# The front part of an attention and MLP block in another order: keys ahead of maxima, idle products in TensorE's waits, 50 maxima at the loop's entry and a lead of five half cycles

## The chip, the core and the metric

The kernel runs on one core of a Trainium2 chip. Time is device microseconds (us) of that core for one launch. TensorE (PE) multiplies, VectorE (DVE) reduces, ScalarE (ACT) takes exponentials and copies, GpSimd (POOL) does elementwise work, SyncE (SP) issues nearly all DMAs. Each engine runs its own queue strictly in the order in which it was written, and so does SP's queue of DMAs.

## The reference

```python
mod = (_silu(c) @ w_mod).reshape(1, 6, 1, -1)          # sa, ca, ga, sb, cb, gb
h = _layernorm(x) * (1 + ca) + sa                       # x: 1 x 2048 x 512
q = (h @ wq) as 32 heads of 16;  k = h @ wk;  v = h @ wv   # one key and value head for all 32
p = softmax(q k^T / 4);  x = x + ga * ((p v) @ wo)
h = _layernorm(x) * (1 + cb) + sb
x = x + gb * (gelu(h @ w1 + b1) @ w2 + b2)              # w1: 512 x 1376
```

All in float32, with wide spreads, so the kernel splits operands into a high and a low part and multiplies three times.

## The kernel before

**Units.** Attention is done in 64 units. A unit is 256 rows of queries and four heads; eight units (u = 8b to 8b+7) make one block b of rows. The four heads stand as two halves s = 0 and 1 of the partitions (rows 0 to 63 and 64 to 127 of the query tile `qst`), with j = 0 and 1 inside a half. Four `qst` buffers turn.

**Two passes over the scores.** The softmax takes the true maximum of each row. So each score is made twice: once as an `m` product (line 516), rows of queries in the partitions, which DVE reduces to a maximum (line 521); and once as an `e` product (line 596), keys in the partitions, from which ACT takes the exponential (line 597). A unit has 32 `m` products and 32 `e` products. The maximum goes into the `e` product itself: it is written, as a high and a low part (`mh`, `ml`), into rows 48 and 49 of each half of `qst`, where the keys `ks` hold -1. Between a unit's last `m` product and its first `e` product lies this chain, `put_max`: DVE reduces the parts (`mm`, line 570) and transposes them (`turned`, 571); POOL gathers and splits them (`mt`, `mh`, `ml`; lines 565, 131, 138); four DMAs (line 560, for s = 1 and then s = 0) bring them into `qst`. The steps are put into the program at set numbers of clock ticks after the last maximum: `reduce` at the start of the next four ticks, `gather` one tick later, `send` four ticks after `reduce`. For u = 8 and 9 `reduce` isn't put off.

**The loop.** After the front part a loop runs over pairs of key tiles, four pairs to a unit. A pair holds eight `e` products, eight `m` products of a later unit, 32 `acc` products (probabilities by values, line 608) and a batch of projection or MLP products (lines 186 and 192); it takes four clock ticks. How many `m` products stand ahead is set by `lead`: at the start of unit u, `first[u + 1] + 4 * LEAD` maxima have been issued, that is all of unit u and 4 * LEAD of the next. `LEAD_0` does the same for the first unit. DMAs are written where the code reaches them: `load_q(u + 1)` (six DMAs that fill another `qst` buffer) when half of a unit's maxima are done, and once per block of rows, in the second unit after the block's end (u = 9, 17, 25, 33, 41, 49, 57), a group that fetches the block's sums and outputs (`rsum`, `drs`, eight `os`, one `x`).

**A wait put early.** A DMA that a product needs soon is noted with `heed`; some ticks later an `acc` product is made to wait for it, so that the `e` products need not. Where no such product comes first, the `e` product itself waits.

**The front part.** Ahead of the loop stand: statistics and normalisation of four blocks of 512 rows (`stats1`, `xhat1`), transposes (`tp`), `mod1` (scale, shift, split on ACT and POOL into `big..H` and `big..L`), the key and value products `kps` of each block (12 products), `kv_out`, `low_k` and `repeat_k`, which fill `ks`, the first two projections of queries, the last part of the modulation (`modl`), and the first maxima. `SLOTS` is the written order: each entry gives how many `m` products to issue (`chunk`) and which steps of other work follow. `FIRST_MAX` gives the order of the first two units' maxima by 512 keys: (unit, key block). Between them an `m` product waits only for its operands and for one of three PSUM banks, which DVE's reduce frees. Before the first `m` product four products that nobody reads (`idle`, `keep_warm`) are already there.

Of the kernel before, what the change touches and what calls it, by code (L numbers as in the profile page):

```python
# [14 lines left out]
P = 128  # L15
# [3 lines left out]

GELU_R = 0.044715 ** 0.5  # L20

LEAD = 6
LEAD_0 = 6
FIRST_MAX = ((0, 0), (1, 0), (0, 1), (1, 1), (0, 2), (0, 3), (1, 2), (1, 3))
SLOTS = ((4, "keys 1", "keys 1"), (2, "keys 1", "keys 1"), (2, "low 1", "heads 2"), (2, "heads 2", "k 1"), (2, "heads 2"), (2, "heads 2", "v 0"),
# [4 lines left out]
MAX_WAIT = (1, 4)  # L30
QBUFS = 4
PREP = 4
# [15 lines left out]
def raw(ap):  # L48
    return ap.bitcast(F32)
# [3 lines left out]
def adaln_mqa_mlp(  # L53
# [270 lines left out]
    wqH = att.tile([P, KD, D], F32R, name="wqH", tag="gH")  # L324
    wqL = att.tile([P, KD, D], F32R, name="wqL", tag="gL")

    def prep_wq(g):
        gs = slice(g * P, (g + 1) * P)
        for j in range(2):
            src = wqf[:, :, gs].rearrange("p k (a j r) -> p k a j r", j=2, r=16)[:, :, :, j, :]  # L330
            dh = wqH[:, :, gs].rearrange("p k (a r j) -> p k a j r", j=2, r=16)[:, :, :, j, :]
            dl = wqL[:, :, gs].rearrange("p k (a r j) -> p k a j r", j=2, r=16)[:, :, :, j, :]
            nc.scalar.copy(dh, src)  # L333
            nc.gpsimd.tensor_tensor(out=dl, in0=src, in1=raw(dh), op=ALU.subtract)

    hts = {}
    hts_stats = {}
# [61 lines left out]
    def repeat_k(b):  # L399
        cols = slice(b * BQ, (b + 1) * BQ)  # L400
        nc.scalar.copy(ks[96:112, cols], raw(ks[32:48, cols]))
# [27 lines left out]

    def qproj(b, g):  # L430

        ps = psum.tile([P, BQ], F32, name=f"qps{b}_{g}", tag="v" if g else "x")
        yield from mm3(ps, qpairs(b, g), 3, 1)
        qH, qL = qtiles(b, g)
        if g == 0:
            nc.scalar.copy(qH, ps)
            nc.vector.tensor_tensor(out=qL, in0=ps, in1=raw(qH), op=ALU.subtract)
        else:
            q32 = pro.tile([P, BQ], F32, name=f"q32_{b}_{g}", tag="h32", bufs=4)
            nc.scalar.copy(q32, ps)  # L440
            split(qH, qL, q32, act, pool)
        send_q(b, g, qH, qL)
        yield -2
# [30 lines left out]
    def load_q(u):  # L474

        b, Q = units[u]
        r0, w = blocks[b]
        qst = qsts[u] = qbufs[u % QBUFS]
        h, g, a0 = r0 // BQ, Q // 2, (Q % 2) * 2
        cols = slice(r0 % BQ, r0 % BQ + w)  # L480
        assert (h, g) in sent

        for s in (1, 0):
            low, high = (dq[h][g][part, a0 + s][:, :, cols] for part in (1, 0))
            n = 6 if s else 8
# [51 lines left out]
    def put_max(u, mx):  # L537

        T = blocks[units[u][0]][1] // P
        qst = qsts[u]
        if not mms:
            for i in range(2):
                mms.append(att.tile([P, 32], F32, name=f"mm{i}"))
                nc.gpsimd.memset(mms[i], 0.0)
        mm = mms[u % 2]
        turned = att.tile([P, 32], F32, name=f"turned{u}", tag="turned", bufs=2)
        if u == 0:
            pad(att, 256, "pad7")  # L550
        mt = att.tile([4 * T, P], F32, name=f"mt{u}", tag="mt", bufs=2)
        mh = att.tile([4 * T, P], F32R, name=f"mh{u}", tag="mh", bufs=2)
        ml = att.tile([4 * T, P], F32R, name=f"ml{u}", tag="ml", bufs=2)

        def send():
            for s in (1, 0):
                for r, src in ((48, mh), (49, ml)):
                    dst = qst[64 * s + r:64 * s + r + 1].rearrange("p j (t n) -> p (j t) n", n=P)
                    ring = nc.scalar if u == 0 and s else nc.sync
                    heed(ring.dma_start(out=raw(dst), in_=raw(src[2 * T * s:2 * T * (s + 1), :].unsqueeze(1))), 5)  # L560
            placed.add(u)

        def gather():
            for g in range(0, P, 32):
                nc.gpsimd.tensor_scalar(out=mt[:, g:g + 32], in0=turned[g:g + 4 * T, :], scalar1=1.0, scalar2=0.0,  # L565
                                        op0=ALU.mult, op1=ALU.add)
            split(mh, ml, mt, nc.gpsimd, nc.gpsimd)

        def reduce():
            nc.vector.tensor_reduce(out=mm[:, :4 * T], in_=mx, axis=AX.X, op=ALU.max)  # L570
            nc.vector.transpose(out=turned, in_=mm)  # L571
            later(MAX_WAIT[0], gather)
            later(MAX_WAIT[1], send)


        if NQ <= u < NQ + 2:
            reduce()
        else:
            later((0 - clock[0]) % 4 + 1, reduce)
# [631 lines left out]

    def chunk(n):
        for _ in range(n):
            mp.step(mp.done % 2)

    act, dve, pool = nc.scalar, nc.vector, nc.gpsimd

# [43 lines left out]
    def q_group():  # L1261
        for i in range(KD):
            next(projections[0])
            if i == KD - 1:
                next(projections.pop(0))
            yield

    def one(fn, *args):
        fn(*args)
        yield  # L1270
# [34 lines left out]
    h1 = heads(1)  # L1305
    run(h1, 2)

    def last_h(t):
        if t == QT - 1:
            run(h1)  # L1310

    stats1(3, last_h)
    load_mods(2)
    repeat_k(0)
    run(xhat1(2, act))
    run(xhat1(3, act))
    work = {"keys 1": keys(1), "heads 2": heads(2), "heads 3": heads(3), "q 1": q_group(), "keys 2": keys(2), "keys 3": keys(3),
            "v 0": one(v_out, 0), "v 1": one(v_out, 1), "v 2": one(v_out, 2), "v 3": one(v_out, 3), "rows": late_rows(),
            "low 1": one(low_k, 1), "low 2": one(low_k, 2), "low 3": one(low_k, 3), "k 1": one(repeat_k, 1), "k 2": one(repeat_k, 2), "k 3": one(repeat_k, 3), "load": one(load_q, 2),
            "wq 1": one(prep_wq, 1), "wq 2": one(prep_wq, 2), "wq 3": one(prep_wq, 3)}  # L1320
    for n, *names in SLOTS:
        chunk(n)
        for name in names:
# [209 lines left out]
```

## Time and profile before

| | |
|---|---|
| median of 3 runs | 1579.97 us (1578.32 to 1580.15) |
| the profiled execution | 1579.71 us, its span 1577.9 us |
| mean granted TensorE clock | 0.997 |
| PE, DVE, ACT, POOL busy | 1554.7, 1403.8, 1204.3, 695.3 us |
| first `m` product, first `e` product | 34.13 us, 79.75 us |

Times on a profile's rows are us from the span's start. A row of the timeline has start, duration, engine, line, operation, output <- inputs, shapes and count; in brackets stands the idle time of the engine just before it and what ended it. In the table of stages a row has the stage, its length, the busy time of PE, weight loads, DVE, ACT and POOL with the number of instructions, the granted clock, and the DMA engines' share and GB/s. Matmuls overlap, so a busy PE isn't PE at its peak.

### The profile page before, as it was taken

To read this page: it belongs to the slowest core of one execution; us is meant where nothing else is said; L and a number is where in the kernel's file an instruction comes from. 1 tells how busy PE (TensorE), PEld (TensorE's weight loads), DVE (VectorE), ACT (ScalarE), POOL (GpSimd) and SP (SyncE) were. 2 spreads that over 40 slices of the span, in tenths; PEclk is the share of its full clock that TensorE was granted. 3 is DMA by queue.
4 is the path that set the end of the run, shared out by engine and by line. 5 is a ranking of instruction groups with operands and counts; after the bars stand their busy time and mean duration, and the time that the engine had idled before them with its cause. 6 is when DMAs were issued, how large, how long until landed. Compare 5 with 4: busy or idle time off the path is not lost.

```text
span 1577.9 us, 43469 instructions
## 1 busy us (share of the span) xinstructions
PE 1554.7 (99%) x17506; PEld 1040.3 (66%) x17506; DVE 1403.8 (89%) x2491; ACT 1204.3 (76%) x2418; POOL 695.3 (44%) x1253
## 2 busy tenths in 40 slices
PE   5999999999999999999999999999999999999999
PEld 3466655667767676667766677676766677676767
DVE  6899999999999999999999999999999999999715
ACT  5477777788877887778877887778877788778863
POOL 4345447447422472245523463334712465224731
PEclk8999999999999999999999999999999999999999
DMA  7236323313021120312112130212112030221341
GB/s 250 83 110 203 121 81 91 100 36 105 20 61 63 59 82 22 93 33 94 46 44 83 44 99 19 76 48 86 56 32 93 27 107 31 62 76 49 100 141 54
DMA packets 80858, 121.48 MB, mean 77 GB/s; under 512 B 16186, under 2 KB 55354, under 8 KB 80400
## 3 DMA queue, kind: packets, MB, share of 16 engines
q1 hardware_dynamic: 80640, 118.70, 23.2%
q8 instruction: 137, 2.24, 0.6%
q14 instruction: 65, 0.53, 0.1%
q10 hardware_dynamic: 16, 0.00, 0.0%
HBM read 91.00 MB, written 26.88 MB: 75 GB/s over the span
## 4 chain that ended last, share of the span: by engine, by line
PE 95%; ACT 3%; DVE 1%; DMA 0%; issue 0%; POOL 0%; SPq 0%; ACTq 0%; DVEq 0%
PE acc L608 32%; PE e L596 20%; PE m L516 18%; PE w1ps L192 8%; PE w2ps L192 6%; PE wops L192 3%; PE qps L192 2%; ACT p L597 2%; PE w2ps L186 1%; PE w1ps L186 1%; PE tp L192 1%; DVE mx L521 1%; PE kps L163 1%; PE wops L186 0%; PE modr L288 0%; DMA xt<-in_A_x_dram 0%
## 5 line engine op out<-in xcount | busy, mean ns | idle before, releaser
L521 DVE TENSOR_REDUCE mx<-m 128x1 f32<-128x512 f32 x2048 | 1270.6, 681 | 98.9 <-PE m L516 90.3
L597 ACT ACTIVATE p<-e 128x512 f32<-128x512 f32 x2048 | 1067.1, 601 | 290.5 <-PE e L596 200.2
L516 PE MATMUL m<-ks,qst 64*128 64x512 f32 x2048 | 828.4, 431 | 6.4 <-DVE ve L204 4.9
L596 PE MATMUL e<-qst,ks 64*128 64x512 f32 x2048 | 731.5, 412 | 2.1 <-ACT wqH L333 1.3
L608 PE MATMUL acc<-p,va 128*32 128x256 f32 x8192 | 548.3, 385 | 0.0
L516 PEld LDWEIGHTS m<-ks,qst 64*128 64x128 f32 x2048 | 367.2, 184 | 103.4 <-DVE mx L521 82.2
L596 PEld LDWEIGHTS e<-qst,ks 64*128 64x128 f32 x2048 | 357.6, 184 | 112.6 <-ACT p L597 102.0
L608 PEld LDWEIGHTS acc<-p,va 128*32 128x32 f32 x8192 | 214.2, 109 | 216.9 <-issue 113.2
L192 PE MATMUL w1ps<-h2H,w1t 64*128 64x256 f32 x1232 | 236.1, 288 | 0.0
L192 PEld LDWEIGHTS w1ps<-h2H,w1t 64*128 64x128 f32 x1232 | 184.0, 185 | 31.7 <-issue 22.2
L565 POOL TENSOR_SCALAR mt<-turned 8x32 f32<-8x32 f32 x256 | 53.2, 208 | 339.0 <-DVE turned L571 326.9
L192 PE MATMUL w1ps<-h2L,w1t 64*128 64x256 f32 x616 | 169.3, 275 | 0.0
L192 PE MATMUL w2ps<-w2H,gH 64*128 64x256 f32 (+1 forms) x556 | 162.3, 296 | 0.0
L192 PE MATMUL w2ps<-w2L,gH 64*128 64x256 f32 (+1 forms) x556 | 156.6, 283 | 0.0
L192 PE MATMUL w2ps<-w2H,gL 64*128 64x256 f32 (+1 forms) x556 | 155.1, 283 | 0.0
L192 PEld LDWEIGHTS w1ps<-h2L,w1t 64*128 64x128 f32 x616 | 113.5, 184 | 0.0
L192 PEld LDWEIGHTS w2ps<-w2H,gH 64*128 64x128 f32 x556 | 101.6, 184 | 10.8 <-issue 4.9
L192 PEld LDWEIGHTS w2ps<-w2H,gL 64*128 64x128 f32 x556 | 101.8, 184 | 2.3
L192 PEld LDWEIGHTS w2ps<-w2L,gH 64*128 64x128 f32 x556 | 102.4, 184 | 1.4
L957 POOL TENSOR_SCALAR tt<-tt 128x256 f32<-128x256 f32 x77 | 31.0, 403 | 144.8 <-ACT tt L956 144.8
L192 PE MATMUL wops<-woH,onH 64*128 64x256 f32 x224 | 67.8, 303 | 0.0
L192 PE MATMUL wops<-woL,onH 64*128 64x256 f32 x224 | 62.2, 277 | 0.0
(233 smaller groups left out, 1602.7 us busy)
## 6 DMA issues: line engine op xcount, KB each, us to landing
w1t<-dw SPq DMA_DIRECT2D x82, 512.0 KB
qst<-dq SPq DMA_DIRECT2D x128, 64.0 KB
do<-oc SPq DMA_DIRECT2D x63, 128.0 KB
dw<-w1s SPq DMA_DIRECT2D x11, 512.0 KB
xt<-in_A_x_dram SPq DMA_DIRECT2D x4, 1024.0 KB
dq<-qH SPq DMA_DIRECT2D x16, 256.0 KB
dq<-qL SPq DMA_DIRECT2D x16, 256.0 KB
qst<-dq SPq DMA_DIRECT2D x128, 32.0 KB
```

Of the source, the lines that this page charges most:

```text
L163: nc.tensor.matmul(ps, a, b_, start=begin and n == 0, stop=end and n == last)
L186: nc.tensor.matmul(ps, a, b_, start=first_, stop=last_)
L192: nc.tensor.matmul(ps, a[rows], b_[rows], start=first_ and s == begin, stop=last_ and s != begin)
L516: nc.tensor.matmul(m, qsts[u][rows, j, t * P:(t + 1) * P], ks[rows, kc * 512:(kc + 1) * 512], start=True, stop=True)
L521: nc.vector.tensor_reduce(out=self.mx[u][:, i, kc:kc + 1], in_=m, axis=AX.X, op=ALU.max)
L565: nc.gpsimd.tensor_scalar(out=mt[:, g:g + 32], in0=turned[g:g + 4 * T, :], scalar1=1.0, scalar2=0.0, op0=ALU.mult, op1=ALU.add)
L596: nc.tensor.matmul(e, ks[rows, kt * P:(kt + 1) * P], rhs, start=True, stop=True)
L597: nc.scalar.activation(ptiles[u, K][:, j, s, :], e, AF.Exp, scale=0.25)
L608: ins = nc.tensor.matmul(accs[u][32 * cidx:32 * cidx + 32, :], va[:, kt, :], rhs, start=kt == 0, stop=kt == NKT - 1)
L957: nc.gpsimd.tensor_scalar(out=tt, in0=tt, scalar1=1.0, scalar2=1.0, op0=ALU.mult, op1=ALU.add)
```

## The change

Four things change together.

1. The order of the front part: `SLOTS` and `FIRST_MAX` are new. Unit 0's maxima go ahead of unit 1's; the first sixteen `m` products come four of a half at a time; the key products of the blocks stand ahead of the maxima that don't need them. The second projection of queries moves from the end of the front part to the wait before the first `m` product, and its weights are split on POOL alone; block 3's `xhat1` moves from ACT to DVE; unit 0's `gather` goes from POOL to DVE; `load_q` of units 0 and 1 takes s = 0 first.
2. Products that nobody reads (`warm`) are put between the first maxima: 12, and then 1 or 2 at a time, 23 in all.
3. The loop is entered with 50 maxima instead of 56 (`LEAD_0` 4.5).
4. `LEAD` is 5 instead of 6.

```diff
-LEAD = 6
-LEAD_0 = 6
-FIRST_MAX = ((0, 0), (1, 0), (0, 1), (1, 1), (0, 2), (0, 3), (1, 2), (1, 3))
-SLOTS = ((4, "keys 1", "keys 1"), (2, "keys 1", "keys 1"), (2, "low 1", "heads 2"), (2, "heads 2", "k 1"), (2, "heads 2"), (2, "heads 2", "v 0"),
...
+LEAD = 5
+LEAD_0 = 4.5
+FIRST_MAX = ((0, 0), (1, 0), (0, 1), (0, 2), (0, 3), (1, 1), (1, 2), (1, 3))
+SLOTS = ((3, "warm"), (1, "keys 1", "warm"), (2, "keys 1", "x 3", "warm"), (2, "keys 1", "x 3", "warm"), (2, "keys 1", "x 3", "warm"),
...
+IDLE = (12, 1, 2, 2, 2, 1, 1, 1, 1)
@@ prep_wq
-    def prep_wq(g):
+    def prep_wq(g, eng=nc.scalar):
...
-            nc.scalar.copy(dh, src)
-            nc.gpsimd.tensor_tensor(out=dl, in0=src, in1=raw(dh), op=ALU.subtract)
+            split(dh, dl, src, eng, nc.gpsimd)
@@ load_q
+        if u < 2:
+            for s in (0, 1):
+                low, high = (dq[h][g][part, a0 + s][:, :, cols] for part in (1, 0))
+                nc.sync.dma_start(out=raw(qst[64 * s + 16:64 * s + 48]), in_=high.unsqueeze(0).to_broadcast([2, 16, 2, w]))
+                nc.sync.dma_start(out=raw(qst[64 * s:64 * s + 16]), in_=low)
+            return
@@ put_max: send, gather
-                    ring = nc.scalar if u == 0 and s else nc.sync
+                    ring = nc.scalar if u == 0 and s == 0 else nc.sync
...
+            eng = nc.gpsimd if u else nc.vector
...
-            split(mh, ml, mt, nc.gpsimd, nc.gpsimd)
+            split(mh, ml, mt, eng, eng)
@@ chunk
-            mp.step(mp.done % 2)
+            mp.step(mp.done // (4 if mp.done < 16 else 2 if mp.done < CH * (NKC + 1) else 1) % 2)
@@ new
+    def warm():
+        for i, n in enumerate(IDLE):
+            ps = psum.tile([P, BQ], F32, name=f"warm{i}", tag="x" if i else "v")
+            for k in range(n):
+                nc.tensor.matmul(ps, wkH[:, 0, :], wkH.rearrange("p k n -> p (k n)"), start=k == 0, stop=k == n - 1)
+            idles.append(ps)
+            yield
@@ the front's steps
+    group = q_group()
+
     def last_h(t):
         if t == QT - 1:
+            run(h1, 1)
+            run(group, KD - 1)
             run(h1)
...
+    run(group)
     run(xhat1(2, act))
-    run(xhat1(3, act))
```

**TensorE's queue at the first maxima.** Before: the transposes of block 1 (`tp`), the first four `m` products of unit 0 (names: unit, j, t, key block and half, without their first number), and the keys of block 1 (`kps`).

```order
L370 MATMUL tp_2_406<-ident,xt_145 128x128 x4
L370 MATMUL tp_3_415<-ident,xt_145 128x128 x4
L516 MATMUL m_0_0_0_0_447<-ks,qst_157 128x512
L516 MATMUL m_0_0_0_1_450<-ks,qst_157 128x512
L516 MATMUL m_0_1_0_0_453<-ks,qst_157 128x512
L516 MATMUL m_0_1_0_1_456<-ks,qst_157 128x512
L163 MATMUL kps_459<-big1H,wkH 128x512
```

The same place after, from the last transposes on; the second projection (`qps_1`) began with nine more products just ahead of these rows.

```order
L372 MATMUL tp_3_429<-ident,xt_145 128x128 x4
L166 MATMUL qps_1_419<-h0H,wqH 128x512
L166 MATMUL qps_1_419<-h0H,wqL 128x512
L166 MATMUL qps_1_419<-h0L,wqH 128x512
L524 MATMUL m_0_0_0_0_468<-ks,qst_157 128x512
L524 MATMUL m_0_1_0_0_471<-ks,qst_157 128x512
L524 MATMUL m_1_0_0_0_474<-ks,qst_157 128x512
L1281 MATMUL warm_477<-wkH 128x512 x12
L524 MATMUL m_1_1_0_0_490<-ks,qst_157 128x512
L166 MATMUL kps_493<-big1H,wkH 128x512
```

The first four maxima are now all of half 0, twelve products that nobody reads stand between the third and the fourth, and the projection stands ahead of them.

**DVE's queue at the end of unit 0's maxima.** Before:

```order
L521 TENSOR_REDUCE mx_446<-m_1_1_3_1_768 128x1
L570 TENSOR_REDUCE mm_771<-mx_446 128x8
L571 STREAM_TRANSPOSE turned_775<-mm_771 128x32
L521 TENSOR_REDUCE mx_498<-m_0_0_2_0_811 128x1
L521 TENSOR_REDUCE mx_498<-m_0_0_2_1_814 128x1
```

After, with the gather on DVE:

```order
L529 TENSOR_REDUCE mx_467<-m_1_1_3_1_785 128x1
L579 TENSOR_REDUCE mm_788<-mx_467 128x8
L580 STREAM_TRANSPOSE turned_792<-mm_788 128x32
L574 TENSOR_SCALAR mt_795<-turned_792 8x32 x4
L138 CAST mh_796<-mt_795 8x128
L141 TENSOR_TENSOR ml_797<-mt_795,mh_796 8x128
L529 TENSOR_REDUCE mx_525<-m_0_0_1_0_810 128x1
```

Six small instructions came into DVE's queue behind unit 0's 40th reduce (before, behind the 48th, there were none).

**SP's queue ahead of unit 33.** `mh33` and `ml33` are that unit's maxima, bound for `qst1`; `qst3<-dq` and `qst3<-dz` are `load_q(35)`; `os3` and `x1_3` belong to the fetch of block 3. Before, behind `drs3<-rsum3` and four `os3`:

```order
L560 DMA qst1_158<-mh33_13366 1x4x128
L560 DMA qst1_158<-ml33_13367 1x4x128
L560 DMA qst1_158<-mh33_13366 1x4x128
L560 DMA qst1_158<-ml33_13367 1x4x128
L1005 DMA out_0_dram<-ot2_0_0_256_13447 128x256
L486 DMA qst3_160<-dq_2_1_96 16x2x256
L487 DMA qst3_160<-dq_2_1_96 32x2x256
L489 DMA qst3_160<-dz_103 2x512
L486 DMA qst3_160<-dq_2_1_96 16x2x256
L487 DMA qst3_160<-dq_2_1_96 32x2x256
L489 DMA qst3_160<-dz_103 2x512
L746 DMA os3_0_13470<-do3_116 128x1x256
```

After, behind the same `drs3<-rsum3` and four `os3`, then `out_0_dram` and four more `os3`:

```order
L793 DMA x1_3_13590<-in_A_x_dram 128x2x512
L494 DMA qst3_160<-dq_2_1_96 16x2x256
L495 DMA qst3_160<-dq_2_1_96 32x2x256
L497 DMA qst3_160<-dz_103 2x512
L494 DMA qst3_160<-dq_2_1_96 16x2x256
L495 DMA qst3_160<-dq_2_1_96 32x2x256
L497 DMA qst3_160<-dz_103 2x512
L568 DMA qst1_158<-mh33_13452 1x4x128
L568 DMA qst1_158<-ml33_13453 1x4x128
L568 DMA qst1_158<-mh33_13452 1x4x128
L568 DMA qst1_158<-ml33_13453 1x4x128
L630 DMA do4_117<-oc32_13739 128x256
```

The four DMAs of the maxima went behind twelve others (one `out`, four `os`, one `x`, six of `load_q`), to the end of the group; the same holds at u = 25, 41, 49 and 57, and at u = 17 with no `out` in the group.

More of the change, by code (lines that the diff above doesn't have):

```diff
@@ L20 @@
 GELU_R = 0.044715 ** 0.5
-LEAD = 6
-LEAD_0 = 6
-FIRST_MAX = ((0, 0), (1, 0), (0, 1), (1, 1), (0, 2), (0, 3), (1, 2), (1, 3))
-SLOTS = ((4, "keys 1", "keys 1"), (2, "keys 1", "keys 1"), (2, "low 1", "heads 2"), (2, "heads 2", "k 1"), (2, "heads 2"), (2, "heads 2", "v 0"),
[4 rows of a table removed]
+LEAD = 5
+LEAD_0 = 4.5
+FIRST_MAX = ((0, 0), (1, 0), (0, 1), (0, 2), (0, 3), (1, 1), (1, 2), (1, 3))
+SLOTS = ((3, "warm"), (1, "keys 1", "warm"), (2, "keys 1", "x 3", "warm"), (2, "keys 1", "x 3", "warm"), (2, "keys 1", "x 3", "warm"),
[5 rows of a table added]
+         (2, "rows"), (2, "rows", "load"), (2, "rows"), (2, "rows"), (2, ))
+IDLE = (12, 1, 2, 2, 2, 1, 1, 1, 1)
 MAX_WAIT = (1, 4)
@@ L430, in qproj @@
     def qproj(b, g):
-        ps = psum.tile([P, BQ], F32, name=f"qps{b}_{g}", tag="v" if g else "x")
+        ps = psum.tile([P, BQ], F32, name=f"qps{b}_{g}", tag="x")
         yield from mm3(ps, qpairs(b, g), 3, 1)
@@ L563, in gather @@
         def gather():
+            eng = nc.gpsimd if u else nc.vector
             for g in range(0, P, 32):
-                nc.gpsimd.tensor_scalar(out=mt[:, g:g + 32], in0=turned[g:g + 4 * T, :], scalar1=1.0, scalar2=0.0,
-                                        op0=ALU.mult, op1=ALU.add)
-            split(mh, ml, mt, nc.gpsimd, nc.gpsimd)
+                eng.tensor_scalar(out=mt[:, g:g + 32], in0=turned[g:g + 4 * T, :], scalar1=1.0, scalar2=0.0,
+                                  op0=ALU.mult, op1=ALU.add)
+            split(mh, ml, mt, eng, eng)
         def reduce():
@@ L1295, in first_q @@
             run(q_group())
+            prep_wq(1, pool)
             load_q(0)
@@ L1314, in adaln_mqa_mlp @@
     repeat_k(0)
+    run(group)
     run(xhat1(2, act))
-    run(xhat1(3, act))
-    work = {"keys 1": keys(1), "heads 2": heads(2), "heads 3": heads(3), "q 1": q_group(), "keys 2": keys(2), "keys 3": keys(3),
+    work = {"keys 1": keys(1), "heads 2": heads(2), "heads 3": heads(3), "x 3": xhat1(3, dve), "warm": warm(), "keys 2": keys(2), "keys 3": keys(3),
             "v 0": one(v_out, 0), "v 1": one(v_out, 1), "v 2": one(v_out, 2), "v 3": one(v_out, 3), "rows": late_rows(),
             "low 1": one(low_k, 1), "low 2": one(low_k, 2), "low 3": one(low_k, 3), "k 1": one(repeat_k, 1), "k 2": one(repeat_k, 2), "k 3": one(repeat_k, 3), "load": one(load_q, 2),
-            "wq 1": one(prep_wq, 1), "wq 2": one(prep_wq, 2), "wq 3": one(prep_wq, 3)}
+            "wq 2": one(prep_wq, 2), "wq 3": one(prep_wq, 3)}
     for n, *names in SLOTS:
```

9 rows, old and new, of the table SLOTS are left out of this document.

## The prediction

> **What bounds the kernel now.** I read the page's busy times, then the table of stages, then the timelines of the front part, last SP's queue in the loop.
>
> ```profile
> PE 1554.7 (99%) x17506; PEld 1040.3 (66%) x17506; DVE 1403.8 (89%) x2491; ACT 1204.3 (76%) x2418; POOL 695.3 (44%) x1253
> ...
> 44.00:80.00 36.00, 33.78 (x161) 16.98 (x160) 32.66 (x54) 19.24 (x37) 16.86 (x24) 1.00 0.14 48
> 800.00:1200.00 400.00, 399.76 (x4811) 272.88 (x4808) 371.15 (x649) 317.19 (x642) 164.48 (x317) 1.00 0.19 61
> ```
>
> In the loop (800 to 1200) PE is busy for 399.76 of 400 us: TensorE's queue sets the pace, and any time in which it stands still there is added to the end. In the front part (44 to 80) DVE is the busiest for its rate, 32.66 of 36, and PE's few products wait for its reduces. So the front part is shortened by giving DVE no gaps, and the loop is lengthened by any new wait of PE.
>
> **The front part.** PE's first maximum and the loop's first `e` product stand at
>
> ```profile
> 28.61 0.66 PE L370 MATMUL tp<-ident,xt 128*128 128x128 f32 x4 [1.25 <-ACT h L376]
> ...
> 34.13 1.19 PE L516 MATMUL m<-ks,qst 64*128 64x512 f32 x3 [4.87 <-DVE ve L204]
> ...
> 79.75 0.59 PE L596 MATMUL e<-qst,ks 64*128 64x512 f32 x2 [1.32 <-ACT wqH L333]
> ```
>
> and DVE's side of it is
>
> ```profile
> 11.28 1.92 DVE L363 TENSOR_SCALAR xt<-xt,mv,rs 128x512 f32<-128x512 f32 x4 [1.15 <-POOL rs L206]
> ...
> 33.92 0.17 DVE L204 TENSOR_SCALAR ve<-mv 128x4 f32<-128x4 f32 x1
> 34.93 2.48 DVE L521 TENSOR_REDUCE mx<-m 128x1 f32<-128x512 f32 x4 [0.85 <-PE m L516]
> 40.09 1.29 DVE L521 TENSOR_REDUCE mx<-m 128x1 f32<-128x512 f32 x2 [2.67 <-PE m L516]
> 42.88 1.29 DVE L521 TENSOR_REDUCE mx<-m 128x1 f32<-128x512 f32 x2 [1.51 <-PE m L516]
> 44.25 0.68 DVE L397 TENSOR_TENSOR ks<-kps,ks 16x512 fp32r<-16x512 f32 x1
> ...
> 74.03 0.19 DVE L570 TENSOR_REDUCE mm<-mx 128x8 f32<-128x32 f32 x1
> 74.25 0.21 DVE L571 STREAM_TRANSPOSE turned<-mm 128x32 f32<-128x32 f32 x1
> ```
>
> DVE can begin reducing at 34.1 (33.92 + 0.17): its queue ahead of that is the same after. From there a reduce takes 0.62 (2.48 / 4). Before, 56 reduces (34.7), three low parts of keys (2.0) and 0.4 stand between 34.1 and 79.75, so 45.65 - 37.1 = 8.5 us are waits: 0.85, 2.67 and 1.51 of them in the three rows above.
>
> After, DVE's work from 34.1 is 50 x 0.62 = 31.0; block 3's normalisation 1.9 (1.92 for the four of block 0); low parts 2.0; `mm` and `turned` 0.4; and the gather, which no row shows on DVE. POOL needs 1.9 for it (row below: from 74.55 to 76.47), and six DVE instructions as long as `turned` are 1.3; I take 1.2. Sum 36.5. The early gaps go: maxima of half 0 need only the first half of `qst`, three are issued before DVE is free, and `warm` products keep the clock. What is late next is POOL, since block 2's and block 3's keys are asked for sooner:
>
> ```profile
> 47.70 3.73 POOL L138 TENSOR_TENSOR big2L<-h,big2H 128x512 fp32r<-128x512 f32 x3
> ...
> 74.55 1.02 POOL L565 TENSOR_SCALAR mt<-turned 8x32 f32<-8x32 f32 x4 [0.47 <-DVE turned L571]
> ...
> 76.02 0.45 POOL L138 TENSOR_TENSOR ml<-mt,mh 8x128 fp32r<-8x128 f32 x1
> 57.74 1.17 ACT L391 CAST ks<-kps 48x512 fp32r<-48x512 f32 x2 [2.72 <-PE kps L163]
> 58.92 0.58 ACT L392 COPY vt<-kps 32x512 f32<-32x512 f32 x1
> ```
>
> A block's split costs POOL four times 1.24 and a cast of half that, 5.6 us. On PE the fourth maximum goes at 34.95 and each of the four slots behind it holds two maxima, three key products and one or two `warm`, about 1.6 us, so block 1's last key product comes near 40.7 (before, half clock held it back, below); ACT's copies and first `h` and cast bring POOL's start to about 43.9, its end to 49.5; key products, ACT's 1.75 and DVE's low part follow at 52.2, where DVE had done its work by 50.4: a wait of 1.8. Block 3 in the same way: ACT's first `h` after its copies near 53, POOL's end near 58.8, low part near 61.5, a wait of 1.9. So the 50th reduce ends at 34.1 + 36.5 + 3.7 = 74.3. PE runs up to two reduces ahead of it (three banks), so the first `e` product could go at 73.1. Its own chain is no longer: unit 0's maxima are complete at 67, and gather (1.0 to `mh`, `ml`), two DMAs on ACT's queue and the landing follow:
>
> ```profile
> 75.97 1.51 ACTq L560 DMA_DIRECT2D qst<-mh  x1
> 77.58 0.59 ACTq L560 DMA_DIRECT2D qst<-ml  x1
> ```
>
> 1.0 + 2.2 + 1.6 (78.17 to 79.75) = 4.8, at 71.8. First `e` at 73.2 instead of 79.75: -6.5. Ends: no wait for POOL -10.0; waits as long as all of before's -2.
>
> The 23 `warm` products cost 23 x 0.23 = 5.3 us of PE (0.23 is the step from one key product to the next at full clock):
>
> ```profile
> 22.99 0.39 PE L163 MATMUL kps<-h0H,wkH 128*128 128x512 f32 x1
> 23.22 0.39 PE L163 MATMUL kps<-h0H,wkL 128*128 128x512 f32 x1
> ```
>
> The first 12 (2.8 us) stand while the fourth maximum waits for the first reduce (34.8); the others stand in slots where PE has about 1.6 us of work to DVE's 1.7. Cover gone, they would cost up to 5.3 at PE, inside the -2. The moved projection (12 products, 2.8 us) fills the 4.87 us gap, at nothing; its DMAs go ahead of the last `wml` load, into an idle SP. `prep_wq(1)` on POOL lies in POOL's idle time before block 1's split. ACT gains back block 3's normalisation.
>
> **The loop's extra products.** Six more `m` products, beside other products on the other half of the array: 0 to 6 x 0.23 = 1.4; I take 0.5.
>
> **The lead.** By the program's order, unit u's last maximum now stands 19 `e` products ahead of its first `e` product (25 before), `turned` 13 (21 before), the sends 5 (13 before). Eight `e` products are one pair, a quarter of a unit. In an ordinary unit that is covered (unit 32, then its first `e`):
>
> ```profile
> 788.59 0.21 DVE L571 STREAM_TRANSPOSE turned<-mm 128x32 f32<-128x32 f32 x1
> ...
> 792.38 0.57 SPq L560 DMA_DIRECT2D qst<-ml  x1
> ...
> 802.18 0.50 PE L596 MATMUL e<-qst,ks 64*128 64x512 f32 x1
> ```
>
> The unit lasts from 802.18 to 824.55 (the next unit's first `e`, below), 22.4 us, so a pair is 5.6: the 13.4 us from `turned` to `e` become 7.8. Gather and four issues take 4.15 (788.80 to 792.95), the landing 1.2 (below): 2.4 us to spare. Not so at u = 17, 25, 33, 41, 49, 57. There SP issues a group without a pause, unit 33's:
>
> ```profile
> 814.04 0.34 SPq L734 DMA_DIRECT2D drs<-rsum  x1
> 814.43 0.64 SPq L746 DMA_DIRECT2D os<-do  x1
> 815.56 0.59 SPq L748 DMA_DIRECT2D os<-drs  x1
> ...
> 819.53 0.57 SPq L560 DMA_DIRECT2D qst<-ml  x1
> ...
> 826.89 0.47 SPq L784 DMA_DIRECT2D x<-in_A_x_dram  x1
> ```
>
> ```profile
> 824.55 0.50 PE L596 MATMUL e<-qst,ks 64*128 64x512 f32 x1
> ```
>
> It starts when DVE has inverted the sums (814.04), a point that moves with the loop and not with the lead, and holds 21 DMAs until 827.36. The same 21 stand there after, but the maxima's four are now the last: they would be issued by 827.36 instead of 820.10. `os<-drs` waited from 814.38 to 815.56 for the DMA before it, so a landing takes 1.2. The first `e` of unit 33 (half 0, whose pair is sent last) wants them at 824.55: 827.36 + 1.2 - 824.55 = 4.0 us late. No `acc` product waits earlier any more; the `e` product itself does, and behind it in TensorE's queue stand all `m`, `e`, `acc` and batch products, with DVE and ACT run dry behind those. Units 17 and 57 (end of group, first `e`):
>
> ```profile
> 465.67 0.47 SPq L784 DMA_DIRECT2D x<-in_A_x_dram  x1
> ...
> 462.04 0.49 PE L596 MATMUL e<-qst,ks 64*128 64x512 f32 x1
> ```
>
> ```profile
> 1371.62 0.47 SPq L784 DMA_DIRECT2D x<-in_A_x_dram  x1
> ...
> 1369.09 0.50 PE L596 MATMUL e<-qst,ks 64*128 64x512 f32 x1
> ```
>
> 5.3 and 4.2. Mean of the three 4.5, six units: +27. Low end, if half 1's pair decided (two issues, 1.25, sooner): 19.5; high end, with the 1.6 landing: 29.5.
>
> **The clock after such a wait.** Before, the one long gap of PE (4.87, up to 34.13) had this behind it:
>
> ```profile
> 29.00:31.00 2.00, 0.26 (x3) 0.02 (x1) 1.97 (x4) 1.97 (x4) 1.72 (x2) 1.00 0.17 36
> 31.00:32.00 1.00, 0.00 (x0) 0.00 (x0) 0.69 (x1) 0.97 (x3) 0.92 (x2) 0.75 0.21 72
> 36.00:41.00 5.00, 5.00 (x12) 2.93 (x11) 2.33 (x5) 2.94 (x5) 0.00 (x0) 0.50 1.03 387
> 41.00:42.00 1.00, 1.00 (x4) 0.85 (x3) 0.37 (x1) 0.00 (x0) 0.00 (x0) 0.63 1.03 422
> ```
>
> Half clock from 31.5 to 41.7, so 7.6 us of work at half speed after the gap ended: 3.8 us lost at most. Gaps of 4.0 to 5.3 are of that kind, but dense work follows at once, where in the front PE still waited until 36.4. Per unit 0 to 3.8; I take the middle, 1.9: +11 (0 to 23). [...]
>
> **Sum.** 1579.71 (the profiled execution, 0.26 below the median, which is nothing here) - 6.5 + 0.5 + 27 + 11 = 1611.7.
>
> **The rivals.**
> - *The front's gain alone, faster:* 1579.7 - 6.5 + 0.5 = 1573.7. It decides if SP clears the group 4 to 5 us sooner than now, so that the four sends land before the first `e`. For it: in ordinary units there is room. Against: in the rows nothing paused in that group but for one landing. 0.14.
> - *Waits, but the clock holds:* 1601 (1589 to 1604). For it: the one gap with half clock behind it had another 1.25 us of idle just ahead (the row at 28.61); PE in the loop is full on both sides. 0.25.
> - *Waits, and each pays the full row:* 1624 (1620 to 1628). [...] 0.13.
> - *Waits of about 1 us each,* if the `e` product comes late for other reasons: they eat the front's gain, no change. 0.03.
> - *The clock isn't kept in the front,* since `warm` stands behind the first three maxima and PE may idle before them: 3 us more in any case above.
>
> **Numbers.** Waits with some loss of clock, 1604 to 1620: 0.45, the likeliest, 1612. The range 1588 to 1628 takes in both neighbours and leaves out the faster case. Within 0.2% (3.2 us) is about what a measurement of this kernel can't tell from no change. Faster 0.14, same 0.03, slower 0.83.
>
> **What would show it.** Right: first `e` near 73; granted clock 1.00 from 31 to 45; PE idle for 4 to 5 us at the first `e` of u = 17, 25, 33, 41, 49, 57, released by a DMA into `qst`, with SP's group ending just before; a stage behind some of them with a clock below 1. Wrong: no idle on PE between 100 and 1480 us (then the lead costs nothing), a first `e` later than 77 (then DVE's gaps were only moved), or waits in ordinary units too.

## The result, and the profile after

The changed kernel takes 1654.07 us (median of 4 runs, 1650.50 to 1656.24) against 1580.06 before: a ratio of 1.0468, with a 95% interval of 1.0445 to 1.0491. It is slower by 74 us where 32 were forecast; the direction was right, the size was not, and the time lies above the stated range (1588 to 1628). The profiled execution took 1652.25 us, its span 1650.2. One profiled execution further below (the first run with the loads behind the sends) took 5702 us where the others of its kernel took 1610 to 1621; it is left out, and what slowed it isn't known.

The engines' row of the page (busy us, share of the span), and the longest of TensorE's waits (us in total, times, longest), after:

```profile
PE 1587.7 (96%) x17529; PEld 1054.6 (64%) x17529; DVE 1411.6 (86%) x2501; ACT 1202.1 (73%) x2412; POOL 694.5 (42%) x1249
```

```profile
PE e L605 <- DMA qst<-ml: 40.8, 13, 6.8
PE modr L291 <- DVE st L201: 8.9, 1, 8.9
PE m L524 <- DVE ks L399: 2.6, 1, 2.6
PE acc L617 <- DMA qst<-dq: 1.8, 1, 1.8
```

Before, no `e` product waited for the maxima's transfers; now 13 do, for 40.8 us. PE's busy time has grown by 33 us as well, although its rows hold only 23 products more. Most of that is the clock: within the span it stands at half for 71.7 us, against 10.2 before, and half of the difference is 31 us. The table of stages (length, busy PE, weight loads, DVE, ACT, POOL, then the granted clock) shows the first and largest piece of it, in the front part, and TensorE's timeline shows where it begins and ends:

```profile
57.00:89.00 32.00, 29.12 (x90) 12.41 (x91) 18.36 (x35) 8.01 (x18) 8.62 (x13) 0.52 0.10 29
```

```profile
56.77 0.47 PE L524 MATMUL m<-ks,qst 64*128 64x512 f32 x1 [0.95 <-ACT big3H L136]
...
72.31 1.22 PE L524 MATMUL m<-ks,qst 64*128 64x512 f32 x2 [2.56 <-DVE ks L399]
...
89.03 0.40 PE L605 MATMUL e<-qst,ks 64*128 64x512 f32 x2
```

The loop's first `e` comes at 89.03, not at 73.2 as forecast, nor at 79.75 as before. Behind a gap of PE of only 0.95 us the clock fell to half and stayed there for 30.7 us.

In the loop the place is the one that was forecast. SP's queue around unit 17, then TensorE and the stages behind:

```profile
469.16 0.33 SPq L743 DMA_DIRECT2D drs<-rsum  x1
...
475.42 0.46 SPq L793 DMA_DIRECT2D x<-in_A_x_dram  x1
475.99 0.62 SPq L494 DMA_DIRECT2D qst<-dq  x1
...
479.24 0.45 SPq L497 DMA_DIRECT2D qst<-dz  x1
479.99 0.66 SPq L568 DMA_DIRECT2D qst<-mh  x1
...
482.60 0.57 SPq L568 DMA_DIRECT2D qst<-ml  x1
```

```profile
485.06 0.76 PE L605 MATMUL e<-qst,ks 64*128 64x512 f32 x1 [5.45 <-DMA qst<-ml]
```

```profile
484.00:490.00 6.00, 4.95 (x31) 2.89 (x33) 2.66 (x4) 2.26 (x5) 0.00 (x0) 0.50 0.00 0
490.00:491.00 1.00, 1.00 (x8) 0.90 (x10) 0.36 (x1) 0.68 (x2) 0.00 (x0) 0.60 0.00 0
491.00:500.00 9.00, 9.00 (x92) 5.26 (x88) 8.29 (x16) 7.18 (x16) 2.30 (x7) 1.00 0.09 31
```

The group, the `x` transfer and the six loads for another unit stand ahead of the maxima's four sends. TensorE stands idle for 5.45 us until they have landed, and the clock is at half from 484.0 to 490.8, of which the first 1.1 us fall into the wait. SP also stood still at the sends themselves. At unit 25, where that was longest, its waits were:

```profile
SPq L568 <- DMA x<-in_A_x_dram: 1.7, 1, 1.7
SPq L568 <- DMA os<-drs: 0.6, 1, 0.6
```

At all six units SP waited at a send until the `x` transfer had landed (0.2 to 1.7 us). By the trace's records that send is counted on the semaphore that the `x` transfer used before it (number 110 at unit 25), and SP waits for that semaphore first, there until 671.98. So the sends came late by their place in the queue and by landings of what was issued ahead of them.

Where the time went can be read from the starts of each unit's first `e` product in the two timelines. How far after lags behind before:

| up to the first `e` of | lag, us | grown by |
|---|---|---|
| unit 0 (front part) | 9.28 | 9.28 |
| unit 16 | 17.45 | 8.17 (units 3, 5, 10 and 14 most: 1.3, 1.0, 2.6, 1.1) |
| units 17, 25, 33, 41, 49, 57 | | 5.56, 6.29, 5.84, 6.37, 6.84, 4.92: 35.8 |
| the units right behind those | | 2.10, 1.35, 1.95, 1.58, 1.76, 2.16: 10.9 |
| all others from 19 on | | 7.9 |
| the last `e` | 72.08 | |

The sends went behind the loads not only in the group: the same order stands at units 5 to 7 and at all from 11 to 61 but 18, and before at none of them. Unit 30's, with TensorE's wait:

```profile
771.98 11.74 SPq L787 DMA_DIRECT2D w1t<-dw  x3
783.77 0.62 SPq L494 DMA_DIRECT2D qst<-dq  x1
...
787.57 0.64 SPq L568 DMA_DIRECT2D qst<-mh  x1
...
789.59 0.57 SPq L568 DMA_DIRECT2D qst<-ml  x1
```

```profile
791.60 0.47 PE L605 MATMUL e<-qst,ks 64*128 64x512 f32 x1 [0.87 <-DMA qst<-ml]
```

### The profile page after: what moved, and what is told of

The parts are those of the page before. It is cut to its first block, busy times and chain, and to the rows that moved or that the text cites. A ratio compares the mean times of both kernels' runs of the same rounds, so it can differ in the third digit from the quotient of the medians.

```text
span 1650.2 us, 43684 instructions
## 1 busy us (share of the span) xinstructions
PE 1587.7 (96%) x17529; PEld 1054.6 (64%) x17529; DVE 1411.6 (86%) x2501; ACT 1202.1 (73%) x2412; POOL 694.5 (42%) x1249
## 4 chain that ended last, share of the span: by engine, by line
PE 72%; POOL 9%; DMA 6%; issue 5%; DVE 4%; ACT 2%; SPq 2%; POOLq 0%; DVEq 0%
PE acc L617 24%; PE e L605 15%; PE m L524 15%; PE w2ps L195 5%; PE w1ps L195 4%; DVE mx L529 3%; PE wops L195 3%; DMA qst<-ml 2%; ACT p L606 1%; PE w2ps L189 1%; PE qps L195 1%; DMA os<-drs 1%; POOL tt L967 1%; POOL z L977 1%; POOL tt L976 1%
## 5 line engine op out<-in xcount | busy, mean ns | idle before, releaser
L524 PE MATMUL m<-ks,qst 64*128 64x512 f32 x2048 | 843.1, 437 | 5.2 <-DVE ks L399 2.6
L605 PE MATMUL e<-qst,ks 64*128 64x512 f32 x2048 | 738.4, 414 | 41.5 <-DMA qst<-ml 40.8
L524 PEld LDWEIGHTS m<-ks,qst 64*128 64x128 f32 x2048 | 373.5, 186 | 110.2 <-DVE mx L529 89.7
L195 PE MATMUL w1ps<-h2H,w1t 64*128 64x256 f32 x1232 | 239.5, 289 | 0.0
L1017 POOL TENSOR_TENSOR ot<-ot,x 128x256 f32<-128x256 f32 x24 | 17.6, 732 | 247.1 <-ACT ot L1016 247.1
```

Of the source, the lines that this page charges most:

```text
L195: nc.tensor.matmul(ps, a[rows], b_[rows], start=first_ and s == begin, stop=last_ and s != begin)
L524: nc.tensor.matmul(m, qsts[u][rows, j, t * P:(t + 1) * P], ks[rows, kc * 512:(kc + 1) * 512], start=True, stop=True)
L605: nc.tensor.matmul(e, ks[rows, kt * P:(kt + 1) * P], rhs, start=True, stop=True)
L1017: later(1, lambda: nc.gpsimd.tensor_tensor(out=ot[:, cols], in0=ot[:, cols], in1=x1[:, t, cols], op=ALU.add))
```

## The experiments

Each was run beside the kernel before on the same chip (medians of before 1580.3 to 1581.4). Times are medians, ratios are to the kernel before, with 95% intervals.

### The front part and the lead apart

**The new front part with the old lead.**

```diff
 (changed kernel)
-LEAD = 5
+LEAD = 6
```

> The changed kernel with LEAD back at 6: its front part alone. In the changed kernel's trace the loop's first e stands at 89.03 us (79.75 before) with the granted clock at 0.5 from 57.3 to 88.0, and the rest of the time came in the loop. Theory (front part worse by 9.3, the lead does all the rest): first e at 89, half clock again from about 57 to 88, no wait of PE for qst at any unit's first e, about 1580 + 9.3 = 1589 us (1586 to 1592). Rival (the prediction's sum, the front gains and what was seen in the front belongs to the lead): first e near 73, 1574 us.

Measured: 1598.38 us, 1.0107 times before (1.0086 to 1.0128). First `e` at 89.1, half clock from 57.5 to 88.2: the front part is worse by 9.4 whatever the lead. Neither the theory's range nor the rival's holds it. The theory missed 9 us, 8.2 of them at unit 3 by the lags of its first `e` and the next unit's:

```profile
145.69 0.57 SPq L1145 DMA_DIRECT2D dw<-w1s  x1
157.24 0.38 SPq L1136 DMA_DIRECT2D w1f<-in_B_w_dram  x1
157.72 0.61 SPq L494 DMA_DIRECT2D qst<-dq  x1
...
161.49 0.63 SPq L568 DMA_DIRECT2D qst<-mh  x1
...
163.48 0.57 SPq L568 DMA_DIRECT2D qst<-ml  x1
```

```profile
164.75 0.76 PE L605 MATMUL e<-qst,ks 64*128 64x512 f32 x1 [5.43 <-DMA qst<-ml]
```

SP stands still for 11 us in front of a weight load (`w1f`), until POOL has cleared its buffer (from 156.70 to 157.22), and then issues six loads ahead of the sends. With lead 5 and 50 maxima those loads happen to come behind the sends, so that the changed kernel waits only 0.87 there.

**The new lead with the old front part.**

```diff
 (kernel before)
-LEAD = 6
+LEAD = 5
 LEAD_0 = 6
```

> The kernel before with LEAD 5 alone: old front part. Theory (the lead's cost does not hang on the front part): first e at 79.75, PE idle 5 to 7 us at the first e of units 17, 25, 33, 41, 49, 57 (36 us), 11 us of half clock behind them, some 16 us in small steps at other units: 1580 + 62 = 1642 us (1636 to 1646). Rival (the small steps come from the changed start of the loop, only the six waits from the lead): 1580 + 47 = 1627 us. The prediction's own sum for the lead: 1618 us.

Measured: 1654.32 us, 1.0462 (1.0444 to 1.0479). It is all of the change's cost, and 12 more than expected: the six waits as told, and unit 3's wait (6.56) with the loads ahead of the sends, as in the run above. The two parts don't add up (18 + 74 against 74), mostly because each alone pays some 8 to 9 us at unit 3 (wait and half clock, read from the lags of its first `e` and the next unit's) and the two together only 1.9.

### The front part's clock

**More products that nobody reads.** In the later slots, where the change had none. The last five groups of them write to another PSUM bank (tag `v`), here and in the runs built on this one.

```diff
 (changed kernel)
-IDLE = (12, 1, 2, 2, 2, 1, 1, 1, 1)
+IDLE = (12, 1, 2, 2, 2, 1, 1, 1, 1, 4, 1, 1, 1, 8, 1, 1, 1, 1)
 SLOTS: "warm" added to the four slots with "heads 3" behind "low 2", to the one with "low 3", and to the four behind
```

> The changed kernel with 19 more warm products in the front part's later slots, where it had none (4, 1, 1, 1 behind block 2's keys, 8 in the slot that waits for block 3's keys, 1 in each of four slots behind). Theory (the half clock from 57.3 on is what the front part lost): the clock stays at 1.00 up to the loop, first e at 79 to 81 instead of 89.0, about 1654 - 9 = 1645 us (1642 to 1648). Rival (the chain of block 3's keys through ACT, POOL and DVE is late whatever the clock): first e at 86 to 89, 1651 to 1656 us. The prediction's sum for the front part at full clock: first e at 73.2, 1638 us.

> Both edits, LEAD 6 and the 19 more warm products: the new front part with the clock kept and the old lead. Theory: first e at 79 to 81 and no waits in the loop, 1578 to 1583 us, no different from before. Rival (keys late whatever the clock): 1586 to 1590 us. The prediction's sum: 1574 us.

Measured: with lead 5, 1650.34 us (1.0444, 1.0428 to 1.0459); with lead 6, 1593.81 (1.0085, 1.0070 to 1.0100). First `e` at 81.98 and 82.00 in place of 89.0 and 89.1: 7 us were the clock. In the medians 3.7 and 4.6 of them came through. In the run with lead 5 unit 9's wait for its query loads (2.0) now brought 3.4 us of half clock at 296, and the lag grew by 5.1 at unit 10 instead of 2.6. With lead 6 unit 3's wait stayed (5.25); the expectations of these two runs didn't have it yet. So the theory was right that the clock was most of the loss, but not that it would now stay at 1.00: it was still at half from 71.0 to 77.8 and from 70.7 to 77.6. Its totals did not hold either.

**The clock kept throughout.** Six products more.

```diff
 (the kernel above with LEAD 6)
-IDLE = (..., 4, 1, 1, 1, 8, 1, 1, 1, 1)
+IDLE = (..., 4, 1, 1, 1, 8, 3, 3, 2, 2)
```

> e4_front_warm (new front part, LEAD 6, 19 more warm products) with 6 further ones in the four slots behind block 3's keys, where the clock halved from 70.7 to 77.6. Theory (that stretch cost some 2 us, the rest of the front part's delay is not the clock): clock 1.00 throughout, first e at 80 (79.5 to 81), 1592 us (1590 to 1593.5). Rival (the clock is all that the front part lacks): first e at 74 to 76, 1587 us.

Measured: 1593.50 us (1.0079, 1.0063 to 1.0095), first `e` at 82.09. Taking away the last stretch of half clock gained nothing, against the theory's 2 us (or the six products cost what it gained); and the clock isn't all that the front part lacks, against the rival. At full clock

```profile
50.00:82.00 32.00, 30.18 (x139) 15.27 (x140) 22.78 (x41) 11.48 (x22) 10.17 (x14) 1.00 0.07 27
```

the front part is still 2.3 us behind the old one. What DVE waits for, in groups of its instructions up to unit 0's last reduce (busy, mean ns, then idle before them and what ended it), first of the changed kernel, then of this one:

```profile
L529 DVE TENSOR_REDUCE mx<-m 128x1 f32<-128x512 f32 x40 | 25.8, 685 | 12.3 <-PE m L524 12.2
...
L399 DVE TENSOR_TENSOR ks<-kps,ks 16x512 fp32r<-16x512 f32 x3 | 2.0, 683 | 3.4 <-ACT vt L394 3.4
```

```profile
L529 DVE TENSOR_REDUCE mx<-m 128x1 f32<-128x512 f32 x40 | 25.8, 686 | 8.6 <-PE m L524 8.4
...
L399 DVE TENSOR_TENSOR ks<-kps,ks 16x512 fp32r<-16x512 f32 x3 | 2.0, 683 | 2.7 <-PE warm L1281 2.0 <-ACT vt L394 0.7
```

15.7 us of waits, 11.3 at full clock. Up to the 50th reduce, where the forecast's sum ends, they are 19.4 and 12.1; the forecast had 3.7. Six of those at full clock, 3.8 us together, are like this one of the changed kernel, in slots that hold one maximum and three key products: a step of 1.32, of which DVE works 0.69.

```profile
49.88 0.69 DVE L529 TENSOR_REDUCE mx<-m 128x1 f32<-128x512 f32 x1 [0.63 <-PE m L524]
```

**Block 3's heads sooner.** They go beside block 2's keys, so that block 3's keys begin one slot behind those.

```diff
 (LEAD 6; warm products in the later slots as above, in other numbers)
-(1, "keys 2"), (1, "keys 2"), (1, "keys 2"), (1, "keys 2"),
-(1, "low 2", "heads 3"), (2, "heads 3", "k 2"), (2, "heads 3", "v 1"), (2, "heads 3"),
-(2, "keys 3"), (1, "keys 3"), (1, "keys 3"), (1, "keys 3"),
+(1, "keys 2", "heads 3"), (1, "keys 2", "heads 3"), (1, "keys 2", "heads 3"), (1, "keys 2", "heads 3"),
+(1, "low 2", "v 1", "warm"), (2, "k 2", "keys 3"), (2, "keys 3"), (2, "keys 3"),
+(2, "keys 3"), (3, "warm"),
```

> The same with block 3's heads put beside block 2's keys, and block 3's keys two to a slot with maxima, one step earlier (the four slots that held the heads alone go). Theory (at full clock the front part waits for block 3's keys, which stand behind block 2's in TensorE's order, and for one maximum to a slot of three key products): block 3's low keys on DVE at 62 to 63 instead of 67.1, first e at 77 to 78, 1589 us (1587 to 1591). Rival (the order of the heads is no matter, ACT and POOL need the time): first e at 80 or later, 1592 to 1594 us.

Measured: 1591.00 us (1.0066, 1.0048 to 1.0084), first `e` at 79.72, block 3's low keys at 64.73. The time is at the end of the theory's range, first `e` and low keys lie between theory and rival: 2.4 us come with that order, and the front part is then level with the old one. The other 6.5 us to the forecast's 73.2 aren't laid to a single place by these runs.

### The six waits

**The loads behind the sends.**

```diff
 (changed kernel)
-                    load_q(u + 1)
+                    later(2, lambda: load_q(u + 1))
```

> The changed kernel with the six transfers that load the next unit's queries put off by two half steps, so that SP issues them behind the four sends of the maxima instead of ahead of them. Theory (the waits at units 17, 25, 33, 41, 49 and 57 are SP's queue, and in it the loads that lead 5 moves ahead of the sends): unit 17's sends end 4.0 us sooner, so its wait of 5.45 becomes 1.5; the six waits fall from 35.3 to about 11.5 us, no wait is long enough for half clock (another 10.9 us), and the small waits behind the batch weights' transfers go (some 6 us): 1654 - 41 = 1613 us (1608 to 1620). Rival (the sends are late by the gather or by slow landing, the order on SP is no matter): 1650 to 1656 us. Second rival: the loads, now late, make other products wait, and half of the gain is given back: 1630 us.

> The same kernel as e5_loads_behind, for a trace of an undisturbed execution: the one profiled there took 5702 us, 3.6 times as long as its timed runs (1610 to 1621). Theory: about 1617 us, waits of PE at the six units of 1 to 2.5 us instead of 5 to 7, no half clock behind them.

Measured: 1616.99, 1610.05 and 1620.62 us in the first's timed runs (1.0223, 1.0195 to 1.0252), 1617.58 in the second (its profile is the one used). Of the 41 us expected 37 came. SP's queue at unit 17, and the product that waits:

```profile
469.69 0.47 SPq L793 DMA_DIRECT2D x<-in_A_x_dram  x1
470.27 0.67 SPq L568 DMA_DIRECT2D qst<-mh  x1
...
472.11 0.57 SPq L568 DMA_DIRECT2D qst<-mh  x1
474.29 0.57 SPq L568 DMA_DIRECT2D qst<-ml  x1
474.91 0.63 SPq L494 DMA_DIRECT2D qst<-dq  x1
```

```profile
476.04 0.46 PE L605 MATMUL e<-qst,ks 64*128 64x512 f32 x1 [1.74 <-DMA qst<-ml]
```

All `e` waits fell from 40.8 to 18.3 us. The six are now 1.7 to 4.0 and not 1.5, and five of them, of 2.7 to 4.0, still brought half clock, against the expectation. At unit 17 SP stood still between two sends (472.68 to 474.29), in its waits for an earlier `os<-do` to land. At the other five the sends were issued one behind the other and landed late. Unit 25's, right behind the `x` transfer, and the product that waits:

```profile
653.38 0.46 SPq L793 DMA_DIRECT2D x<-in_A_x_dram  x1
653.95 0.66 SPq L568 DMA_DIRECT2D qst<-mh  x1
...
656.03 0.57 SPq L568 DMA_DIRECT2D qst<-ml  x1
```

```profile
660.03 0.76 PE L605 MATMUL e<-qst,ks 64*128 64x512 f32 x1 [2.79 <-DMA qst<-ml]
```

At these five the first `e` came 3.1 to 4.2 us behind the last issue, against 1.2 to 2.2 in the changed kernel. By the semaphores' records the `x` transfer was complete at 659.40 here and the last send at 659.89, and at all five the last send was complete 0.2 to 0.9 us after `x`. So the first rival's slow landing is a part of what is left: with the loads moved, the sends stand next behind `x`.

**The sends ahead of half the group, at these six units alone.**

```diff
 (changed kernel)
-        if NQ <= u < NQ + 2:
+        if NQ <= u < NQ + 2 or u % NQ == 1 and u > NQ:
             reduce()
```

> The changed kernel with the maxima of units 17, 25, 33, 41, 49 and 57 alone gathered at once (the reduce over the maxima not put off to the next step), so that SP issues their four sends ahead of the second half of its group. Theory (those six waits and their half clocks are one cause, apart from the front part and the small waits): the six waits and the half clock behind them vanish, 1654 - 35.8 - 10.9 = 1607 us (1604 to 1611); the small waits at other units stay. Rival (the second half of the group, four places later, makes the norm and the batch products wait): 1615 to 1625 us.

Measured: 1619.27 us (1.0242, 1.0224 to 1.0260). It is outside the theory's range and inside the rival's. The six waits and every half clock behind them are gone, but the lag grows by 1.0 to 2.2 us in the unit behind each, 9 us in all. Some 3 us of that stand in waits of `acc` products for query loads, not for the norm or the batch as the rival had it; the rest isn't traced to a wait. TensorE's waits for `qst` in the whole run:

```profile
PE e L605 <- DMA qst<-ml: 6.4, 9, 1.1
PE acc L617 <- DMA qst<-dq: 4.8, 8, 1.4
```

**A lead in between.**

```diff
-LEAD = 5
+LEAD = 5.5
```

> The changed kernel with LEAD 5.5. Theory (the sends go by whole steps and stand at the same e product as with 5; only the loads move two e products up and still stand ahead of them): the six waits stay as they are, unit 3 waits 5 us more since its loads now come ahead of its sends: 1655 us (1650 to 1663). Rival (the cost falls with the lead, e products by e products): half of the lead's cost, about 1620 us.

Measured: 1663.53 us (1.0527, 1.0511 to 1.0543), worse than 5, as the theory said, and just past the end of its range. The sends go at whole steps of four ticks and stay where they were; only the loads move ahead of them at unit 3 (wait 5.79). The cost doesn't fall with the lead; what counts is who stands ahead of whom on SP.

**All mended at lead 5.** Both edits and the first 19 warm products.

> The changed kernel, lead still 5, with three edits together: the 19 more warm products, the loads put behind the sends, and the maxima of units 17, 25, 33, 41, 49 and 57 gathered at once. Theory (front clock, loads ahead of the sends, and the six groups are all that the change cost): first e at 82 as with the warm products alone (+2.3), none of the six waits, none of the small ones, 1 to 1.5 us left behind each of the six groups: 1580 + 2.3 + 8 = 1590 us (1584 to 1596). Rival (the shorter lead costs by itself, wherever the sends stand): over 1605 us.

Measured: 1589.44 us (1.0059, 1.0046 to 1.0073), as expected. Of 13 waits for the maxima one is left:

```profile
PE e L605 <- DMA qst<-ml: 0.9, 1, 0.9
```

So 65 of the 74 us are named and taken away without touching the lead. Lead 6 with the same front part takes longer (1593.81), but some 8 us of its time are unit 3's wait and the half clock behind it, which no run here cured without a price elsewhere. Outside the front part and units 3 and 4 the last `e` lags by 6.1 here and by 3.1 with lead 6, so a small price of the shorter lead itself isn't ruled out.

**The loads behind at lead 6.** The same edit of `load_q` on the kernel with lead 6 and 19 warm products.

> LEAD 6 with the 19 more warm products (1593.8 us) and the loads put behind the sends. Theory (unit 3's wait of 5.25 us there is SP standing at a weight load until 157 us and then issuing the six loads ahead of the sends): the sends land 4 us sooner, the wait becomes 1.3, no half clock behind it (2.7): 1593.8 - 6.7 = 1587 us (1584 to 1589). Rival (unit 3 waits for something else than its place on SP): 1592 to 1595 us.

Measured: 1596.87 us (1.0104, 1.0091 to 1.0118), outside both expectations. Unit 3's wait did shrink from 5.25 to 0.87, without half clock. But the lag grows by 2.3 at unit 10 and by 0.6 to 1.9 behind each of the six groups, 9.5 in all, where the loads now stand behind the group; `acc` products wait 2.3 us for them. At lead 6 the sends already stood ahead of the group; moving the loads cures one place and hurts seven.

### The clock in the old front part

```diff
 (kernel before)
+    keep_warm(20)
     for n, *names in SLOTS:
```

> The kernel before with 20 products that nobody reads ahead of its first maximum, where TensorE stood idle for 4.87 us and the clock halved from 31.5 to 41.7. Theory (the clock counts in the front part): clock at 1.00 throughout, DVE's waits of 2.67 and 1.51 us at 37.4 and 41.4 shrink to under 0.7 each, first e at 77 instead of 79.75, 1577.5 us (1576 to 1578.5). Rival (the chain of keys is what the front part waits for later on, so the early gain is lost again): 1579.5 to 1580.5 us.

Measured: 1578.19 us, 0.9986 (0.9977 to 0.9995, eleven runs). The gain of 2.2 us is within the theory's range. In the profiled execution, though, first `e` came only at 79.2: block 1's low keys were done 3.5 us sooner, and that was lost again beside half clock from 64.0 to 70.8 and from 81.0 to 84.4. So eleven products more were added:

```diff
+IDLE = (2, 1, 1, 2, 5)
-(2, "heads 2", "k 1"), (2, "heads 2"), (2, "heads 2", "v 0"),
+(2, "heads 2", "k 1", "warm"), (2, "heads 2", "warm"), (2, "heads 2", "v 0", "warm"),
...
-(0, "v 2"), (2, "q 1"), (2, "q 1"), (2, "q 1"),
+(0, "v 2"), (2, "q 1"), (2, "q 1", "warm"), (2, "q 1"),
...
+(0, "warm")
```

> The kernel before with the 20 products ahead of its first maximum and 11 more: 2, 1, 1 beside block 2's heads, 2 beside the late projection, 5 behind the last slot. In the profiled execution of the kernel with the 20 alone the gain of 3.5 us up to block 1's low keys held until 62 us and was lost to half clock from 64.0 to 70.8 and 81.0 to 84.4. Theory (with the clock kept there too the gain reaches the end): first e at 76.5 to 77.5, 1577 us (1575.5 to 1578.3). Rival (TensorE's added products stand in its way): 1578.5 to 1581 us.

Measured: 1578.11 us, 0.9988 (0.9979 to 0.9997). The same stretch before, and with these products, and the first `e` of the latter:

```profile
28.00:78.00 50.00, 43.27 (x188) 22.53 (x188) 41.05 (x71) 29.76 (x49) 21.32 (x31) 0.90 0.30 104
```

```profile
28.00:78.00 50.00, 48.52 (x223) 26.77 (x224) 41.53 (x71) 31.38 (x55) 22.59 (x32) 1.00 0.30 105
```

```profile
77.38 0.59 PE L597 MATMUL e<-qst,ks 64*128 64x512 f32 x2
```

First `e` 2.4 us sooner, and the loop keeps the lead to its end (2.1 at the last `e`). Both versions are faster than the kernel before by some 0.1%, with intervals that end just under 1; between the two there is no difference that these runs show.

## Why the prediction was right, and where it was wrong

- **Slower, by waits at six named units:** right, and shown. PE stands idle at the first `e` of units 17, 25, 33, 41, 49 and 57, released by a DMA into `qst`, with SP's group just ahead; putting the sends ahead of half the group takes the six away.
- **Their size, +27:** measured 35.8. The step that failed was "827.36 + 1.2": a group of 21 issues as long after as before, and a landing of 1.2. After, the stretch from `drs` to the last send took 14.0 to 15.7 us (13.3 counted), and the first `e` followed the last issue by 1.2 to 2.2. SP stood at the sends until the `x` transfer (0.2 to 1.7 us, all six) and an `os<-drs` (0.2 to 0.8, five of them) had landed; at unit 49 it also waited 1.8 us for `drs`, and at unit 33 one issue, of an `os<-drs`, took 2.16 us, the other three 0.57 to 0.59. The forecast saw one landing in the group, that of `drs`, and put the others at nothing.
- **The clock behind them, +11:** measured 10.9. That half clock follows these waits was right, at all six; the middle between the row's ends was taken without a row for it, so that the sizes agree is in part luck. Each wait brought 6.8 us of half clock, of which 1.1 (unit 17) to 3.4 us (unit 25) fell into the wait itself: 1.35 to 2.16 us of lag were left.
- **"2.4 us to spare" in an ordinary unit:** right for the gather and the four issues alone, and wrong as a claim that nothing else happens there. Some 16 us grew outside the front part and the six pairs of units. Waits of 0.6 to 1.8 at eight units (3, 9, 14, 30, 38, 53, 54, 61) are 7 of it. At the last six of these the sends stand behind six loads, and the loads mostly behind a weight transfer; at unit 3 the sends stand right behind one; at unit 9 an `acc` product waits for the loads themselves. With the order mended only unit 3's is left, at 0.9. The rest is steps of 1 us or less. I had costed the loads' move ahead of the sends only in the group; it happened in nearly every unit from 11 on.
- **The front part, -6.5:** measured +9.3, and the largest miss. The step that failed is "36.5 + 3.7": the 3.7 us of DVE's waits. Up to the 50th reduce, which ended at 90.5 and not at 74.3, they were 19.4, and DVE's work was 37.6 (36.5 in the forecast). The forecast counted two waits, one for POOL behind each of two splits, and these came near it (0.7 and 2.7). What it put at nothing, DVE's waits for maxima from PE, was the other 16. At full clock all waits were 12.1: PE paced the slots with one maximum beside three key products, and also the early slots priced at "about 1.6 us", which took 2.02 (their maxima start at 35.94, 37.97, 39.99 and 42.02). Half clock, from 57.3 on, added 7 us to the first `e`. What was forecast for the first maxima did come: the clock stood at 1.00 until 57.3. The forecast named "clock not kept" for the place ahead of the first maxima, priced it at 3, and didn't look at the slots behind them, which have no warm products.
- **Six more `m` products, +0.5:** not to be told apart; nothing speaks against it.
- **The rivals:** that the clock holds in the loop, or that the six waits don't come, is refuted by the rows above. The rival "each pays the full row" would have given a time nearer to the truth for a reason that isn't true: the time it lacks came from the front part and the ordinary units.

Together, against the forecast sum: front part 15.8, six waits 8.8, ordinary units 15.6, clock 0; 40.2 of the 40.5 us between 1611.7 and the profiled 1652.25.

## What to carry to other kernels

A shorter lead isn't paid in distance alone: ask what the moved step now stands behind in every in-order queue, in each place of the program and not only where the queue is fullest; here the order on SP alone was worth 61 us (1650.34 to 1589.44), with the shorter lead kept. Ask also which transfers ahead must have landed before the next one is issued. A slot-by-slot plan of a front part needs the busy time of each engine in each slot, the slower one taken; adding up the work of the one engine that looks full forecasts its waits too small. And a stretch in which PE waits is to be checked for the clock, even if no gap in it is long: here half clock came behind one of 0.95 us, and lasted 30.7.

## What the runs showed of the hardware

The stretches of half clock were of a few lengths. In the front part half clock lasted 10.2 us in the kernel before (31.5 to 41.7) and 30.7 in the changed kernel (57.3 to 88.0); with 20 products ahead of the old front part's first maximum 6.8 and 3.4 (64.0 to 70.8, 81.0 to 84.4). In the changed kernel's loop it came six times, for 6.8 us each, and between the second, third, fourth, fifth and sixth of these (671.7, 862.9, 1054.0, 1245.1 and 1436.3) lie 184.3 us each time. What sets these lengths and distances wasn't shown.

Not only long waits had it behind them. In the changed kernel half clock began during each of the six waits of 4.83 to 6.77 us, and there was none at the eight waits of 0.58 to 1.83 us in the loop. With the loads behind the sends five waits of 2.7 to 4.0 us had it, and with 19 warm products more one of 2.0. In the changed kernel's front part the last gap ahead of 57.3 was one of 0.95 us; PE was busy for 2.45 of the 3.40 us up to there. No experiment changed the use of PE alone, so how little of it brings half clock wasn't shown. Nor was what brings full clock back: from 57.3 to 88.0 PE was busy for 27.82 of 30.7 us, at half clock throughout.
